# A linear recurrence with decay: chunks of 64 with the decay divided out, in place of block levels in chunks of 32

## The chip, the cores and the metric

The kernel runs on one core of a Trainium2 chip. A core has a matrix engine (TensorE, "PE" in the profile; its weight loads are "PEld"), a vector engine (VectorE, "DVE"), a scalar engine (ScalarE, "ACT"), GpSimd ("POOL") and SyncE ("SP"), which here only issues transfers. Each engine works its own list of instructions in order and waits on semaphores for the others. The metric is the device time of one execution in microseconds; less is better.

## The reference

For 4 sequences of 768 tokens and 8 heads of 40 channels, a state of 40 x 40 per head is carried over the tokens. The result of all heads is a row of 320 numbers per token, which then goes through two matrix products with a silu between them.

```python
for t in range(S):                                   # S = 768
    kt, vt, rt = (k[:, :, t], v[:, :, t], r[:, :, t])
    wt, at, bt = (w[:, :, t], a[:, :, t], b[:, :, t])
    y[:, :, t] = np.einsum('bhd,bhde->bhe', rt, state)
    Sa = np.einsum('bhde,bhe->bhd', state, at)
    state_decay = state * wt[:, :, None, :] - np.einsum('bhd,bhe->bhde', Sa, bt)
    state = state_decay + np.einsum('bhd,bhe->bhde', vt, kt)
...
h = x @ w_in                                         # (3072, 320) @ (320, 2048)
g = h * (1.0 / (1.0 + np.exp(-h)))
return (g @ w_out).astype(np.float32)                # (3072, 2048) @ (2048, 320)
```

The decays w are drawn between 0.85 and 0.95. All of it is float32; a float32 matrix product is two instructions on TensorE, a transpose one. The weights arrive as float64 and are put together to float32 on VectorE, nine instructions for each of 22 pieces (lines 126 to 134).

## The kernel before

A **unit** is 128 tokens of one sequence with all 8 heads. Two sequences are worked side by side, so a **group** is two units, and there are 12 groups. Channels lie on partitions, two heads of a pair in one tile (64 rows each, 40 used).

Inside a unit the recurrence is worked in 4 chunks of C = 32 tokens. What token s adds reaches token t through the product of the decays between them. That product is never formed by a quotient: each pair of tokens lies in one pair of sibling blocks of 1, 2, 4, 8 or 16 tokens (five **levels**), and each level has its own scaled copies of a, k and b. So the following stands once per level:

- `level` (lines 179 to 218): score products (line 191, weights of 128 columns), a masked copy on VectorE (line 195), transposes (line 207), and the scaling for the next level on GpSimd (lines 211 to 216);
- `read_level` (lines 365 to 402): products of r with v and u (line 375), a mask (line 382), the product with the keys (line 391), the scaling (line 399) and the sum (line 400).

Between them lie `by_token` (transposes, line 228, and line 232), `inverse` (forward substitution, 31 rows of two VectorE instructions each, lines 256 and 262, for the 64 chunks of two units on 64 partitions, with the scores going through memory before and the inverse after it), `solve` (lines 287 and 294, alternating head by head), and `chunk` (lines 308 to 355), which carries the state over the 4 chunks.

`moe` is the two matrix products (lines 423 and 440) with the sigmoid (line 431) and the product (line 432) for 256 tokens. `weave` spreads two lists of steps over each other: the rest of the group (from `inverse` on) with the `moe` of the group before. What engines do in the end is set by the scheduler, which moves independent instructions.

## Time and profile before

| | before |
|---|---|
| median of 3 runs | 3177.6 us (3167.85 to 3179.37) |
| span of the profiled execution | 3174.8 us |
| PE busy | 2888.6 us, 16992 matmul instructions |
| DVE busy | 1139.0 us |
| ACT busy | 482.0 us |
| POOL busy | 422.5 us |
| mean granted TensorE clock | 0.596 of full speed |

The span is what the profiled execution's instructions cover; it stands 2.8 us under the median. Busy time of PE is a union: overlapping matmuls count once. A row of instructions with "x" gives their number; a clock of 1.00 is 2.4 GHz and of 0.50 is 1.2 GHz.

### The profile page before, as it was taken

What the parts mean: (1) busy time and instruction counts of PE and PEld (TensorE: products, weight loads), DVE (VectorE), ACT (ScalarE), POOL (GpSimd) and SP (SyncE); (2) the same over time, 40 slices, a digit from 0 to 9 for tenths busy, and PEclk for the clock granted to TensorE, in tenths of its full rate; (3) what the DMA queues carried; (4) which work ended last, traced back from release to release, by engine and by line L of the source; (5) the groups of instructions that cost most, each with busy time, mean ns of one, the idle gap of its engine ahead of it and who ended that gap; (6) DMA issues with size and microseconds to landing.
All of it is one profiled execution on the core that took longest, in us unless ns stands there. A gap on an engine that the chain in (4) does not pass through costs nothing.

```text
span 3174.8 us, 40492 instructions
## 1 busy us (share of the span) xinstructions
PE 2888.6 (91%) x16992; PEld 2494.4 (79%) x16992; DVE 1139.0 (36%) x2146; ACT 482.0 (15%) x1058; POOL 422.5 (13%) x714
## 2 busy tenths in 40 slices
PE   8189989989989989998998998998999899899898
PEld 8178868958968968886896895897788689589686
DVE  5935423252251351342324225135034232422512
ACT  1001201111111111110120111111112012011111
POOL 4001101200300200210120030020011012003000
PEclk9555755575585575565566557557557555655757
DMA  3211101000010010000100000001001010000000
GB/s 86 75 40 43 27 11 29 27 11 9 23 36 5 25 36 5 27 27 11 29 27 11 24 22 21 5 25 31 9 27 29 9 29 27 11 20 13 15 1 9
DMA packets 103981, 75.56 MB, mean 24 GB/s; under 512 B 57976, under 2 KB 84344, under 8 KB 103800
## 3 DMA queue, kind: packets, MB, share of 16 engines
q1 hardware_dynamic: 100608, 62.16, 7.2%
q10 hardware_dynamic: 3192, 10.81, 1.2%
q8 instruction: 134, 2.20, 0.3%
q14 instruction: 47, 0.39, 0.0%
HBM read 58.79 MB, written 10.22 MB: 22 GB/s over the span
## 4 chain that ended last, share of the span: by engine, by line
PE 78%; DVE 17%; DMA 2%; SPq 1%; issue 1%; ACT 1%; POOL 0%; DVEq 0%; ACTq 0%; POOLq 0%
PE pm L191 23%; PE pg L336 11%; DVE tmp L256 8%; PE pl L375 7%; DVE XT L262 6%; PE pq L354 6%; PE pc L391 6%; PE pt L207 4%; PE pa L287 4%; PE pu L308 4%; PE pz L294 4%; PE pt L320 3%; PE ph L423 3%; PE pv L232 2%; PE pt L228 2%; DVE gts L432 1%
## 5 line engine op out<-in xcount | busy, mean ns | idle before, releaser
L191 PEld LDWEIGHTS pm<-a,kb 40*128 40x128 f32 x3840 | 733.4, 327 | 49.2 <-issue 28.9
L191 PE MATMUL pm<-a,kb 40*128 40x64 f32 x3840 | 758.1, 419 | 10.6 <-DMA a<-in_aT 9.1
L195 DVE COPY_PREDICATED MM<-mm_s,pm 128x512 f32<-128x512 int32 x240 | 227.5, 949 | 591.9 <-PE pm L191 591.9
L287 PE MATMUL pa<-XTb,at 128*64 128x128 f32 x384 | 132.0, 448 | 244.6 <-DMA XTb<-xd 244.6
L423 PE MATMUL ph<-xt,wi_s 120*128 120x256 f32 (+1 forms) x1152 | 289.0, 408 | 10.1 <-DMA xt<-mid 8.0
L423 PEld LDWEIGHTS ph<-xt,wi_s 120*128 120x128 f32 (+1 forms) x1152 | 224.5, 202 | 70.5 <-DVE gts L432 29.2
L327 POOL TENSOR_TENSOR gw<-G,tot 64x160 f32<-64x160 f32 x192 | 88.6, 461 | 1406.8 <-DVE G L346 1397.9
L256 DVE TENSOR_TENSOR tmp<-XT,mi 64x1 f32<-64x1 f32 (+30 forms) x372 | 272.5, 732 | 8.0 <-issue 0.3
L287 PEld LDWEIGHTS pa<-XTb,at 128*64 128x64 f32 x384 | 55.5, 206 | 263.9 <-issue 250.0
L375 PE MATMUL pl<-r,left 40*64 40x64 f32 x3840 | 245.7, 318 | 14.3 <-ACT left L369 14.3
L214 POOL TENSOR_TENSOR kb<-kb,tot 128x256 f32<-128x256 f32 x240 | 171.8, 716 | 586.2 <-PE pm L191 539.4
L375 PEld LDWEIGHTS pl<-r,left 40*64 40x64 f32 x3840 | 202.9, 216 | 44.3 <-ACT left L369 19.1
L311 DVE TENSOR_TENSOR U<-pu,zv 32x320 f32<-32x320 f32 x96 | 46.8, 487 | 499.7 <-PE pu L308 499.7
L440 PE MATMUL po<-wo_s,gts 128*128 128x320 f32 x768 | 209.7, 434 | 0.3
L346 DVE TENSOR_TENSOR G<-pg,gw 64x160 f32<-64x160 f32 x192 | 61.8, 322 | 399.8 <-PE pg L336 396.7
L336 PEld LDWEIGHTS pg<-v,kq 32*128 32x128 f32 x768 | 170.7, 323 | 31.7 <-issue 31.7
L440 PEld LDWEIGHTS po<-wo_s,gts 128*128 128x128 f32 x768 | 145.3, 190 | 63.1 <-DVE gts L432 4.3
L391 PE MATMUL pc<-lam,kt 128*64 128x64 f32 x1920 | 190.1, 324 | 3.2
L336 PE MATMUL pg<-v,kq 32*128 32x80 f32 x768 | 191.3, 427 | 0.0
L262 DVE TENSOR_REDUCE XT<-tmp 64x1 f32<-64x1 f32 (+30 forms) x372 | 184.2, 495 | 10.8
L354 PE MATMUL pq<-r,gt 128*128 128x32 f32 x768 | 184.1, 404 | 0.0
L336 PE MATMUL pg<-U,kq 32*128 32x80 f32 x768 | 183.5, 417 | 0.0
(63 smaller groups left out, 2689.0 us busy)
## 6 DMA issues: line engine op xcount, KB each, us to landing
kb<-in_bT SPq DMA_DIRECT2D x24, 256.0 KB
kb<-in_kT SPq DMA_DIRECT2D x24, 256.0 KB
a<-in_aT SPq DMA_DIRECT2D x24, 256.0 KB
tot<-in_wT SPq DMA_DIRECT2D x24, 256.0 KB
r<-in_rT SPq DMA_DIRECT2D x24, 256.0 KB
vu<-in_vT SPq DMA_DIRECT2D x24, 256.0 KB
room<-in_w_out ACTq DMA_DIRECT2D x10, 512.0 KB
room<-in_w_in ACTq DMA_DIRECT2D x8, 480.0 KB
```

Source lines behind the costliest of these rows:

```text
L191: nc.tensor.matmul(pm[:, c : c + 64], lhsT=u.kb[R, n, p, :], rhs=a_r[R, p], start=True, stop=True)
L195: nc.vector.copy_predicated(dst, mm_s[:, lv].bitcast(I32).rearrange("p (n l) -> p n l", l=L).unsqueeze(1).to_broadcast([128, H, 64 // L, L ...
L214: nc.gpsimd.tensor_tensor(out=k_l, in0=k_l, in1=totals(u.tot, lv, 1), op=ALU.mult)
L256: nc.vector.tensor_tensor(out=tmp[:, 0:t, 0:t], in0=XT[:, 0:t, 0:t], in1=mi[:, 0:t, t].unsqueeze(1).to_broadcast([NU * H * NC, t, t]), op= ...
L262: nc.vector.tensor_reduce(out=XT[:, 0:t, t], in_=tmp[:, 0:t, 0:t], axis=AX.X, op=ALU.add)
L287: nc.tensor.matmul(pa[DP * j : DP * j + DP, p * TT : p * TT + TT], lhsT=u.at[:, p, DP * j : DP * j + DP], rhs=x, start=True, stop=True,)
L336: nc.tensor.matmul(pg[:, p * 80 : p * 80 + 80], lhsT=u.kq[R, n, p, :], rhs=U[u.n][R, p, :, 0:D] if n else u.v[R, p * 80 : p * 80 + 80], st ...
L354: nc.tensor.matmul(pq[:, p * C : p * C + C], lhsT=gt[:, p, :], rhs=u.r[:, p, R], start=True, stop=True)
L375: nc.tensor.matmul(pl[64 * n : 64 * n + 64, p * 64 : p * 64 + 64], lhsT=left[R, n * P + p, :], rhs=halves(u.r, L)[1][R, p], start=True, st ...
L391: nc.tensor.matmul(pc[DP * j : DP * j + DP, p * 64 : p * 64 + 64], lhsT=u.kt[:, lv, p, DP * j : DP * j + DP], rhs=lam[:, j, p], start=True ...
L423: nc.tensor.matmul(ph[:, 0:T], lhsT=wi_s[0:n, k, f * 128 : f * 128 + 128], rhs=xt[0:n, k, :], start=k == 0, stop=k == 2,)
L440: nc.tensor.matmul(po[u.n][:, 0:DM], lhsT=gts[0][:, f, u.n * TT : u.n * TT + TT], rhs=wo_s[:, f, :], start=f == 0, stop=f == NF - 1,)
```

## The change

The levels go. A chunk is now C = 64 tokens, and a unit is 64 tokens of two sequences (`n` counts 12 steps of 64 tokens, `m` the two pairs of sequences), so that there are 24 units as before and the two sequences of a unit share the 128 partitions where tokens lie on partitions. For each unit a scan on VectorE forms the running product W of the decays, a reciprocal R = 1/W is taken, a is multiplied by W, and k and b by R (`scale`). Then one set of scores (`between`) serves the whole chunk, for b ahead of time and for k in `right`. The inverse of a 64 x 64 triangle is put together from its two 32 x 32 diagonal blocks, which `inverse` solves for four units at once on 128 partitions (6 times in all), and two small products in `merge`. The state is carried once per 64 tokens (`update`), and y is read out by one set of products (`read`, `write`).

Since 1/W could grow too large for other decays, the sums of squares of R and of W go to `chk`. At the end they are compared with 2^80, and if any is not below, a general version of the whole kernel, token by token on VectorE, runs behind a branch (lines 626 to 714 of the changed kernel). The weights' pieces come in another order, 9 of the 22 ahead of the first steps.

```diff
-C = 32
-LEVELS = (1, 2, 4, 8, 16)
-TT = 128
+TT = C = 64
+LIMIT = 2.0**80
...
-    def level(u, lv):
...
-    def read_level(u, lv):
...
+    def between(u, n, name, bufs):
+        s = sb.tile([128, 2, P, C], F32, name=name, bufs=bufs)
+        pm = [bank("pm") for _ in range(2)]
+        for p in range(P):
+            for be in range(2):
+                for j in range(2):
+                    q = P * be + p
+                    J = slice(DP * j, DP * j + DP)
+                    nc.tensor.matmul(
+                        pm[j][C * be : C * be + C, p * C : p * C + C],
+                        lhsT=u.kb[J, q, n, :],
+                        rhs=u.a[J, q, :],
...
+        def scale():
+            u.W = sb.tile([128, Q, C + 1], F32, name="W", bufs=6)
+            nc.vector.tensor_tensor_scan(
...
+            R = w[:, :, 1 : C + 1]
+            nc.vector.reciprocal(R, u.W[:, :, 1 : C + 1])
+            nc.gpsimd.tensor_tensor(out=u.a, in0=u.a, in1=u.W[:, :, 0:C], op=ALU.mult)
+            for n in (1, 0):
+                nc.gpsimd.tensor_tensor(out=u.kb[:, :, n], in0=u.kb[:, :, n], in1=R, op=ALU.mult)
+            junk = sb.tile([128, Q, C], F32, name="yx")
+            c = 2 * (NM * u.n + u.m)
+            nc.scalar.activation(out=junk, in_=R, func=AF.Square, accum_out=chk[:, c : c + 1])
...
     def inverse(md):
...
-        mi = sb.tile([NU * H * NC, C, C], F32, name="mi", tag="mid", bufs=2)
+        mi = sb.tile([128, 32, 32], F32, name="mi")
...
+    def merge(u, xd, zd):
...
     def chain(u, xt):
...
+        def read():
+            u.lam = sb.tile([128, 2, Q, C], F32, name="lam")
+            for j in range(2):
+                J = slice(DP * j, DP * j + DP)
+                pl = bank("pl")
+                for q in range(Q):
+                    nc.tensor.matmul(
+                        pl[:, q * C : q * C + C], lhsT=u.vut[J, q].rearrange("p n t -> p (n t)"), rhs=u.r[J, q, :], start=True, stop=True
+                    )
...
+        return [keys, right, solve] + ([] if last else [update]) + [read, write] + ([] if last else [turn])
...
+    load_w(units[0][0])
+    for u in units[0] + units[1]:
         load(u)
-    behind = load_weights()
-    for g in range(groups):
-        us = units[g]
-        for u in us:
+    ready = load_weights()
+    weave(prepare(0) + prepare(1), ready[0:9])
+    behind = ready[9:]
+    xt = None
+    for n in range(NN):
+        for u in units[n]:
             load_rv(u)
...
+        parts = [chain(u, xt) for u in units[n]]
+        steps = [x for pair in zip(*parts) for x in pair]
+        ahead = prepare(n + 2)
+        cut = len(behind) * 4 // len(steps)
+        weave(steps[0:4], behind[0:cut])
+        weave(steps[4:], behind[cut:], ahead)
+        behind = moe(n, xt)
     weave(behind)
...
+    flag = nc.values_load(bad[0:1, 0:1], min_val=0, max_val=1)
+    with tc.If(flag > 0):
```

The built programs show what becomes of this on the engines. A row is a line of the kernel, the operation, what it writes and reads, the shape of its output, and how many stand in a run. First TensorE before, in a middle group, from the last scores (L191) over `by_token` (L228, L232) and `moe` (L423, L440) to `solve` (L287, L294):

```order
L191 MATMUL pm<-a,kb 128x64 x16
L207 MATMUL pt<-ident,left 128x128 x4
L228 MATMUL pt<-ident,a 128x128 x4
L228 MATMUL pt<-ident,kb 128x128 x8
L232 MATMUL pv<-v,MM_75 128x40 x8
L423 MATMUL ph<-xt,wi_s 128x256 x48
L440 MATMUL po<-wo_s,gts 128x320 x32
L287 MATMUL pa<-XTb_76,at 64x128
L294 MATMUL pz<-mv,XTb_76 128x40
```

And TensorE after, in the second half of a step that has `moe` woven in (L516 and L533 are its two products; L463 is `read`, L476 and L483 are `write`, L284 is `merge`):

```order
L463 MATMUL pl<-r,vut 128x64 x16
L516 MATMUL ph<-xt,wi_s 128x256 x6
L463 MATMUL pl<-r,vut 128x64 x16
L533 MATMUL po<-wo_s,gts 128x320 x8
L476 MATMUL py<-r,GT_92 128x64 x8
L483 MATMUL py<-lam,kt 64x64 x16
L533 MATMUL po<-wo_s,gts 128x320 x4
L476 MATMUL py<-r,GT_93 128x64 x8
L483 MATMUL py<-lam,kt 64x64 x16
L533 MATMUL po<-wo_s,gts 128x320 x20
L516 MATMUL ph<-xt,wi_s 128x256 x46
L284 MATMUL pq<-XT_96,sb 32x32 x8
```

What stood in one piece, 48 and 32 products of `moe` followed by a product that needs the inverse, now stands in pieces of 3 to 8 products between those of the chain, and one long piece of 20 and 46 ahead of `merge`, which needs the inverse.

On the boundary between two steps after, TensorE has the transposes of `turn` (L452) and of `keys` (L341), then the scores (L185) and the products of `right` (L349, L361), with a few products of `moe` (L533):

```order
L483 MATMUL py<-lam,kt 64x64 x15
L452 MATMUL pt<-ident,Gbd_90 128x128 x4
L185 MATMUL pm<-a,kb 64x64 x16
L533 MATMUL po<-wo_s,gts 128x320 x2
L452 MATMUL pt<-ident,Gbd_91 128x128 x8
L533 MATMUL po<-wo_s,gts 128x320 x4
L341 MATMUL pt<-ident,kb 128x128 x16
L185 MATMUL pm<-a,kb 64x64 x16
L349 MATMUL pr<-Gbd_90,a 64x80 x8
L361 MATMUL pr<-v_2870,sk 64x40 x2
```

With the four of L452 that stand just ahead of these rows, 32 transposes lie on one boundary. Before, the nearest to it were the 24 of `by_token`, 12 for each unit with L232 between them.

On VectorE, at the start, the order after is the conversion of the pieces (L135 to L143), the scan and the reciprocal (L204, L213), the rows of the inverse (L247, L253), and only then the first mask of a chain step (L193 into `sk`):

```order
L140 SCALAR_TENSOR_TENSOR room<-room 120x512
L204 SCALAR_TENSOR_TENSOR W<-w,one 128x520
L142 TENSOR_TENSOR room<-room 120x512
L213 RECIPROCAL w<-W 128x8x64
...
L253 TENSOR_REDUCE XI<-tmp 128x31
L139 SCALAR_TENSOR_TENSOR room<-room 128x512
...
L143 ISA wo_s<-room 128x1024
L193 TENSOR_TENSOR sk<-pm,ms 128x256 x4
L436 TENSOR_TENSOR t<-pg,G_88 128x320
```

All 22 pieces stand ahead of that first mask; before, the pieces lay between the masked copies and the rows of the first group.

## Rows read from the trace of the kernel before

**Rows 1.** The page: engines' busy time, and the granted clock in 40 slices.

```profile
PE 2888.6 (91%) x16992; PEld 2494.4 (79%) x16992; DVE 1139.0 (36%) x2146; ACT 482.0 (15%) x1058; POOL 422.5 (13%) x714
...
PEclk9555755575585575565566557557557555655757
```

**Rows 2.** The page: the chain of work that ended last, shares by engine.

```profile
PE 78%; DVE 17%; DMA 2%; SPq 1%; issue 1%; ACT 1%; POOL 0%; DVEq 0%; ACTq 0%; POOLq 0%
```

**Rows 3.** Windows over one group: stretch, busy us of each engine (instructions), clock.

```profile
core 0: us, PE busy (x) PEld busy (x) DVE busy (x) ACT busy (x) POOL busy (x), PEclk, DMA share, GB/s
807.00:871.00 64.00, 64.00 (x320) 60.16 (x319) 16.27 (x18) 10.41 (x25) 18.54 (x29) 0.50 0.02 5
871.00:875.00 4.00, 4.00 (x20) 3.88 (x20) 0.72 (x1) 1.69 (x3) 1.80 (x3) 0.50 0.20 32
875.00:885.00 10.00, 10.00 (x70) 9.38 (x69) 1.27 (x3) 4.22 (x10) 2.98 (x2) 1.00 0.59 185
885.00:920.00 35.00, 34.71 (x138) 25.01 (x136) 32.83 (x69) 5.48 (x15) 0.00 (x0) 1.00 0.02 5
920.00:938.00 18.00, 2.80 (x10) 1.87 (x10) 8.71 (x7) 0.36 (x1) 0.00 (x0) 0.58 0.18 38
948.00:1015.00 67.00, 67.00 (x306) 58.87 (x306) 9.29 (x25) 7.54 (x17) 5.46 (x12) 0.50 0.02 5
1015.00:1050.00 35.00, 33.56 (x452) 28.77 (x454) 13.97 (x36) 8.31 (x15) 0.00 (x0) 0.50 0.10 25
```

**Rows 4.** Groups of instructions by line: busy us, mean ns of one.

```profile
L423 PE MATMUL ph<-xt,wi_s 120*128 120x256 f32 (+1 forms) x1152 | 289.0, 408 | 10.1 <-DMA xt<-mid 8.0 <-DVE gts L432 0.4
L256 DVE TENSOR_TENSOR tmp<-XT,mi 64x1 f32<-64x1 f32 (+30 forms) x372 | 272.5, 732 | 8.0 <-issue 0.3
L195 DVE COPY_PREDICATED MM<-mm_s,pm 128x512 f32<-128x512 int32 x240 | 227.5, 949 | 591.9 <-PE pm L191 591.9
L440 PE MATMUL po<-wo_s,gts 128*128 128x320 f32 x768 | 209.7, 434 | 0.3
L262 DVE TENSOR_REDUCE XT<-tmp 64x1 f32<-64x1 f32 (+30 forms) x372 | 184.2, 495 | 10.8
L382 DVE TENSOR_TENSOR lam<-pl,my_s 128x256 f32<-128x256 f32 x240 | 101.8, 424 | 111.9 <-PE pl L375 110.9
```

**Rows 5.** Timeline of TensorE at the boundary of the two clock levels: start, us, operation.

```profile
873.39 1.82 PE L228 MATMUL pt<-ident,kb 128*128 128x128 f32 x8
875.05 1.87 PE L232 MATMUL pv<-v,MM 128*128 128x40 f32 x16
...
935.20 0.66 PE L287 MATMUL pa<-XTb,at 128*64 128x128 f32 x2 [15.31 <-DMA XTb<-xd]
935.79 0.65 PE L294 MATMUL pz<-mv,XTb 128*128 128x40 f32 x2
936.37 0.69 PE L287 MATMUL pa<-XTb,at 128*64 128x128 f32 x2
```

**Rows 6.** Timeline of TensorE in another group, the same line at the lower level.

```profile
1385.35 3.47 PE L232 MATMUL pv<-v,MM 128*128 128x40 f32 x16
```

**Rows 7.** Windows over the start, of VectorE's instructions on the pieces of the weights.

```profile
0.00:300.00 300.00, 105.99 (x198) 0.66 0.23 65
```

**Rows 8.** TensorE's longest wait: total us, times, longest.

```profile
PE pa L287 <- DMA XTb<-xd: 244.6, 12, 76.6
```

**Rows 9.** Timeline of the end: last products, the transfer of y, the first of `moe`.

```profile
3118.17 12.14 SPq L408 DMA_DIRECT2D xt<-mid  x16
3118.61 1.70 PE L391 MATMUL pc<-lam,kt 128*64 128x64 f32 x16
3131.59 22.89 PE L423 MATMUL ph<-xt,wi_s 80*128 80x256 f32 x90 [0.26 <-DMA xt<-mid]
```

**Rows 10.** Timeline of the start: VectorE's first instruction on a piece.

```profile
9.24 0.43 DVE L126 TENSOR_SCALAR room<-room 120x512 int32<-120x512 int32 x1 [3.06 <-DMA room<-in_w_in]
```

More of the change, by code (lines that the diff above doesn't have):

```diff
@@ L357, in turn_u @@
[L357 to L374 removed]
+            nc.sync.dma_start(xd, XI)
@@ L453, in moe @@
         for f in range(NF):
             steps.append(partial(first, f))
-        for u in units:
+        for m in range(NM):
             for part in range(4):
-                steps.append(partial(second, u, part))
+                steps.append(partial(second, m, part))
         return steps
-    groups = (B // NU) * NT
-    units = [[unit(g, n) for n in range(NU)] for g in range(groups)]
-    for u in units[0]:
-        load(u)
-    behind = load_weights()
-    for g in range(groups):
-        us = units[g]
-        for u in us:
-            load_rv(u)
-        for lv in range(NL):
-            for u in us:
-                level(u, lv)
-        md = dr.tile([NU * H * NC, C, C], F32, name="md", bufs=2)
-        xd = dr.tile([NU * H * NC, C, C], F32, name="xd", bufs=2)
-        for u in us:
-            send_scores(u, md)
-        for u in us:
-            by_token(u)
-        xt = sb.tile([128, 3, NU * TT], F32, name="xt", bufs=2)
-        steps = inverse(md, xd)
-        steps += [partial(solve, u) for u in us]
-        steps += [partial(chunk, u, c) for c in range(NC) for u in us]
-        steps += [partial(turn_u, u) for u in us]
-        for lv in reversed(range(NL)):
-            steps += [partial(read_level, u, lv) for u in us]
-        steps += [partial(send_y, u, xt) for u in us]
-        if g + 1 < groups:
-            steps += [partial(load, u) for u in units[g + 1]]
-        weave(steps, behind)
-        behind = moe(us, xt)
@@ L490, with prepare, begin, do @@
-    weave(behind)
+    units = [[unit(n, m) for m in range(NM)] for n in range(NN)]
+    md = {}
+    def prepare(n):
+        if n >= NN:
+            return []
+        if n % 2 == 0:
+            md[0] = dr.tile([128, 32, 32], F32, name="md", bufs=2)
+        steps = [x for u in units[n] for x in pre(u, md[0])]
+        if n % 2 == 0:
+            return steps
+        box = {}
+        def begin():
+            box["rows"], box["xd"], box["zd"] = inverse(md[0])
+        steps.append(begin)
+        for i in range(32):
+            steps.append(lambda i=i: box["rows"][i]())
+        four = [(u, {}) for k in (n - 1, n) for u in units[k]]
+        for k, i in ((0, 0), (1, 0), (2, 0), (3, 0), (0, 1), (1, 1), (0, 2), (2, 1), (1, 2), (3, 1), (2, 2), (3, 2)):
+            def do(u=four[k][0], b=four[k][1], i=i):
+                if i == 0:
+                    b["s"] = merge(u, box["xd"], box["zd"])
+                b["s"][i]()
+            steps.append(do)
+        return steps
@@ new lines @@
+    weave(behind)
+    bad = const.tile([1, 1], I32, name="bad")
+    ok = sb.tile([128, 2 * NM * NN], F32, name="ok")
+    count = sb.tile([128, 1], F32, name="count")
+    ones = sb.tile([128, 1], F32, name="ones")
+    pb = bank("pb")
+    nc.vector.memset(ones, 1.0)
+    nc.vector.tensor_scalar(out=ok, in0=chk, scalar1=LIMIT, scalar2=None, op0=ALU.is_lt)
+    nc.vector.tensor_reduce(out=count, in_=ok, axis=AX.X, op=ALU.add)
+    nc.tensor.matmul(pb[0:1, 0:1], lhsT=count, rhs=ones, start=True, stop=True)
```

669 lines of the change are left out of this document (411 added, 258 removed).

## The prediction

> **What bounds the kernel now.** I read the page's shares first. TensorE is busy for 2888.6 of 3174.8 us, VectorE for 36% of the span, the others for less [rows 1]; and the chain that ended last lies on TensorE for 78% and on VectorE for 17% [rows 2]. So TensorE's list, in order, is the time, and VectorE counts where TensorE waits for it: it sits idle 244.6 us in 12 waits for the inverse [rows 8]. Next the windows over one group, which split the list by kind of work [rows 3]. The scores of the levels take 64 us with 320 instructions, 200 ns each; the chunks 67 us with 306, 219 ns each; the reading levels 33.56 us with 452, 74 ns each. The three differ little in arithmetic. The first two load weights of 128 columns for every instruction, the third of 64 columns, and alternate between the two halves of the columns. So **an instruction costs by its width: about 219 ns wide, 74 ns narrow**, whatever its product is worth. All three ran at a granted clock of 0.50, that is 1.2 GHz; `moe` ran at 1.00. The clock column is the second thing to see: it rises as the transposes of `by_token` have run, and falls in the window in which TensorE waits for the inverse. L232 shows what it is worth on wide instructions: 16 in 3.47 us at the lower level [rows 6], in 1.87 us at the higher [rows 5], a factor of 0.54.
>
> `moe` takes 289.0 and 209.7 us [rows 4], 499 in all; what is left of TensorE's busy time, 2390 us, is the recurrence.
>
> **The change on TensorE.** By the rows of the built program a unit has 64 score products after (L185), 64 in `merge`, 48 in `right`, 64 in `solve`, 32 in `update` and 32 narrow ones in `write`, counted as instructions: 304 narrow. Wide are 16 transposes, 32 in `read` and 16 in `write`: 64. Before, the recurrence had 15072 instructions, now 24 x 368 = 8832, and most of them narrow.
> - At the lower clock: 304 x 74 ns = 22.5 us and 64 x 219 ns = 14.0 us, 36.5 us a unit, 876 us in all, against 2390.
> - At the higher: the wide 14.0 x 0.54 = 7.6 us. No row shows narrow ones there; their bounds are half (11.3 us) and no gain (22.5 us), and I take 17, the middle. 24.6 us a unit, 590 in all.
> - Narrow products that differ in rows of the array alone, as half of L185 do, are not in the trace either. If these didn't overlap, some 100 a unit would cost up to twice 74 ns, 7 us a unit; if four ran side by side, less than 74. I leave 74.
>
> `moe` stays at 499 us.
>
> **The other engines.** The rows of the inverse cost (272.5 + 184.2) / 12 = 38 us a time [rows 4]; with 128 partitions filled they come 6 times, not 12: 228 us of VectorE gone. The masked copies go (227.5 us). A mask of 128x256 costs 0.42 us [rows 4]; four a unit, two of double size and the rest make some 9 us a unit with the scan and the reciprocal. These two the trace doesn't show: an instruction over 512 elements takes between 0.7 us (0.42 scaled from 256) and the 0.95 us of the masked copy [rows 4], and with twice that for a serial operation I take 1.3 us each. VectorE comes to 24 x 9 + 228 + 79 for `moe` + 106 = about 630 us. It stays under TensorE. The Trainium skill ("VectorE: DVE Perf Modes", First, the fixed hardware budget) says that reciprocal is an iterative divide with a repeat count of 8; an estimate by that page is 4.3 us for 512 elements, which would add some 15 us to the start below and nothing elsewhere. No row here shows it.
>
> **The start loses its cover.** This is the part that speaks against the change. VectorE needs 106 us for the weights [rows 7], which lay beside TensorE's long scores. Now all 22 pieces stand ahead of the first mask of a step in VectorE's order, and so do the first inverse (38), five scans and reciprocals (13), eight masks (3.4); its first piece lands at 9.2 us [rows 10], and the clearing of buffers takes 3. Sum 173 us, in which TensorE only has the scores and merges of four units, 4 x 96 x 74 ns = 28 us.
>
> **Waits.** The transfer of y takes SyncE 12.14 us for a group [rows 9] and `moe` of the same step stands right behind it; 20 to 24 products of 0.54 us each are ahead of it in one kind of step, transposes in the other, which covers most. Changes of shape cost too: L287 and L294, two and two, take 1.17 us for four [rows 5], 292 ns each against 219, or 0.15 us a change, and a step has some 25 more changes than the rows that I took prices from. I put 7 us on each of 11 steps, 77 in all. The wait for the inverse mostly goes, since 40 products of L533 and 92 of L516 (some 34 us) stand ahead of `merge`.
>
> **The end.** From the last narrow product's start to dense `moe` it took 13 us [rows 9]; I take 11 from its end, 3 for the last store, and 5 (a guess) to read the flag and branch past the general version: 19.
>
> **The sum.** 173 + 848 (876 less the 28) + 499 + 77 + 19 = **1616 us with the recurrence at 1.2 GHz**, and with 571 (590 less 19) in place of 848 **1339 us at 2.4 GHz**. Which? In the window 875 to 885 the clock had risen behind 12 transposes and stayed up through L232 [rows 3, 5]; the fall comes where TensorE idles. After the change the long idle is gone, and each step's boundary has 32 transposes, so I expect the higher level for two thirds of the recurrence: 1616 - 185 = 1431. The span stands 2.8 us under the median of the runs, which is nothing here: **1430 us**.
>
> A rule of the Trainium skill speaks against that step: "TensorE: Matmul & The Clock Gate", Part 4, says that transposes don't count as a busy array and don't bring the full clock. By it the boundary would not lift the clock, and the sum would lie near 1616. The trace disagrees: at 875 us the level was 1.00 and only the levels' work and the transposes of L228 stood ahead of it [rows 3, 5].
>
> **Rivals.**
> 1. *The clock stays high and narrow products halve.* For it: no fall in the trace with TensorE at work. Against: long stretches of narrow and wide work stayed at 0.50. Time: 173 + 24 x (7.6 + 11.3) - 14 + 499 + 96 = 1208, up to 1339.
> 2. *The clock stays low,* since the pieces of `moe` are too short between the steps of the chain. The woven part of `moe` then doubles too: 48 and 12 of 96 and 64 products per two steps, 30.7 us, 5.5 times, 169 us. Time 1616 to 1785.
> 3. *VectorE's queue.* In each second step the masks of `read` and the scaling of y stand behind rows of the inverse. TensorE has some 30 us of work ahead of them; if that were not so, up to 38 us in each of 6 steps: 1430 + 228 = 1660 at most. The Trainium skill ("TensorEngine Tiling (Array Packing)", Key Properties) says that a change of tiling mode drains the array, which would work in the same direction; the 0.15 us a change of L287 and L294 agrees, and 46 changes a step by 12 would be 83 us, of which the sum has about half.
> 4. *The other side: the general version runs.* It decides at a sum of squares of 2^80 = 1.2e24. With decays of 0.85 and more, 64 of them give 1/W of at most 33,000, and 512 squares 5.6e11, so the branch should not be taken. If it were, 768 tokens by 9 VectorE operations of some 0.5 us (0.42 for 256 elements, here 400) would add 3500 us: about 5000, slower.
>
> **How the numbers follow.** The mixed clock, 1340 to 1560: 0.5. Rival 1: 0.17. Rival 2: 0.2. Rival 3 alone: 0.1. Rival 4: 0.03. The range takes in rival 1 from its lower end and rivals 2 and 3 to the middle: 1210 to 1700, about 0.8. A difference of 0.5% is what a measurement of this kernel can tell from none; here all cases but the last are far beyond it: faster 0.96, same 0.01, slower 0.03.
>
> **What would show it.** TensorE with about 10750 matmul instructions and still the engine of the last chain; narrow runs (L185, L383, L483) near 74 ns an instruction where the clock is 0.50; a first L516 no sooner than 200 us; a granted clock between 0.7 and 0.9 over the span; no wait over 10 us for the inverse past the start. Wrong would be: a clock near 0.5 throughout, narrow products at over 100 ns, or waits of TensorE for VectorE in every step.

## The result, and the profile after

| | before | after |
|---|---|---|
| median | 3173.74 us (3167.85 to 3179.37) | **1168.44 us** (1157.89 to 1178.94, 4 runs) |
| ratio, 95% interval | | **0.3671** [0.3651, 0.3692] |
| span of the profiled execution | 3174.8 us | 1156.1 us |
| mean granted clock | 0.596 | 0.929 |

The change makes the kernel 2.7 times as fast. The forecast was 1430 us with a range from 1210: the direction is right, the size is not, and the time lies below the whole range, near the lower end of rival 1 (1208). The ratio leaves out the run of 1178.94 us, which counts as a slow one.

The page of the kernel after: busy time, the granted clock in 40 slices, and the chain that ended last. They answer to [rows 1, 2].

```profile
PE 938.7 (81%) x10674; PEld 763.6 (66%) x10674; DVE 622.7 (54%) x1037; ACT 267.7 (23%) x652; POOL 137.4 (12%) x138
...
PEclk9999998799998998997999997998988999979899
...
PE 54%; DVE 25%; SPq 9%; DMA 7%; issue 2%; ACT 1%; POOL 1%; DVEq 0%; ACTq 0%; POOLq 0%
```

TensorE is still first, with 10674 instructions (about 10750 were forecast), but no longer for nine tenths of the span. The clock column is the surprise: before, its digits were mostly 5, now they are 7 to 9.

The windows show where TensorE is idle (columns as in [rows 3]):

```profile
0.00:177.00 177.00, 17.62 (x398) 16.52 (x399) 166.09 (x288) 19.08 (x45) 39.40 (x40) 1.00 0.47 116
177.00:240.00 63.00, 57.05 (x918) 50.19 (x917) 25.75 (x38) 18.09 (x43) 9.47 (x10) 0.81 0.38 93
240.00:520.00 280.00, 263.32 (x3037) 210.82 (x3036) 153.02 (x250) 76.75 (x190) 33.89 (x32) 0.94 0.28 67
520.00:1085.00 565.00, 539.44 (x6020) 439.21 (x6020) 268.28 (x443) 145.94 (x356) 54.60 (x57) 0.92 0.25 61
1085.00:1156.10 71.10, 61.26 (x308) 46.82 (x307) 9.52 (x21) 7.85 (x20) 0.00 (x0) 0.93 0.06 15
```

In the first 177 us VectorE works for 166 and TensorE for 18. After that TensorE idles 48 us up to 1085 (the lengths less the busy times) and 10 us in the last window.

The groups by line, which answer to [rows 4]: seven of TensorE's and four of VectorE's. The "mean ns" of TensorE's rows counts overlapped instructions in full, so the price of one is the busy time divided by the count.

```profile
L516 PE MATMUL ph<-xt,wi_s 120*128 120x256 f32 (+1 forms) x1152 | 305.7, 416 | 44.6 <-DVE gts L525 21.3 <-DMA xt<-yx 20.1 <-issue 1.7
L533 PE MATMUL po<-wo_s,gts 128*128 128x320 f32 x768 | 229.7, 449 | 0.0
L463 PE MATMUL pl<-r,vut 64*128 64x64 f32 x768 | 81.9, 282 | 0.0
L476 PE MATMUL py<-r,GT 128*128 128x64 f32 x384 | 66.8, 348 | 0.0
L185 PE MATMUL pm<-a,kb 64*64 64x64 f32 x1536 | 43.2, 235 | 72.9 <-POOL kb L216 72.9
...
L421 PE MATMUL pg<-vu,kt 128*64 128x40 f32 x704 | 24.2, 230 | 0.7 <-issue 0.7
L401 PE MATMUL pw<-XT,RHS 64*64 64x64 f32 x768 | 21.2, 225 | 0.0
...
L247 DVE TENSOR_TENSOR tmp<-XI,mi 128x1 f32<-128x1 f32 (+30 forms) x186 | 138.6, 745 | 4.2 <-DMA mi<-md 0.7
L253 DVE TENSOR_REDUCE XI<-tmp 128x1 f32<-128x1 f32 (+30 forms) x186 | 93.4, 502 | 3.9
L213 DVE RECIPROCAL w<-W 128x512 f32<-128x512 f32 x24 | 80.3, 3347 | 0.8
...
L204 DVE TENSOR_TENSOR_SCAN W<-w,one 128x520 f32<-128x520 f32 x24 | 30.7, 1278 | 6.6 <-DMA w<-in_wT 6.0 <-DVE sk L193 0.3
```

43.2 us for 1536 products of L185 is 28 ns each, 28 for L401, 34 for L421; the wide L463 and L476 stand at 107 and 174. All nine narrow lines together come to 263 us for 7232 instructions, 36 ns each.

The timeline of TensorE in one step without `moe` (start, us, line); its last row is L476 in another step, one with `moe`:

```profile
684.25 2.29 PE L421 MATMUL pg<-vu,kt 128*64 128x40 f32 x64
686.47 0.69 PE L185 MATMUL pm<-a,kb 64*64 64x64 f32 x32
687.10 6.80 PE L463 MATMUL pl<-r,vut 64*128 64x64 f32 x64
693.83 3.67 PE L476 MATMUL py<-r,GT 128*128 128x64 f32 x16
...
599.90 1.90 PE L476 MATMUL py<-r,GT 128*128 128x64 f32 x16
```

And the windows of the same stretch, for the clock:

```profile
687.00:692.40 5.40, 5.40 (x70) 5.33 (x63) 4.09 (x7) 0.00 (x0) 2.31 (x4) 1.00 0.56 136
692.50:706.10 13.60, 13.60 (x107) 12.68 (x106) 6.48 (x5) 0.59 (x1) 0.02 (x1) 0.50 0.32 74
```

32 products of L185, which go round the four quarters of the array, take 0.69 us, 22 ns each. And the clock falls at 692.5 us although TensorE is busy without a gap in both windows: in the wide run of L463, so that 16 of L476 take 3.67 us and elsewhere 1.90.

### The profile page after: what moved, and what is told of

It is laid out like the page before. It is cut to its first block, busy times and chain, and to the rows that moved or that the text cites. A ratio compares the mean times of both kernels' runs of the same rounds, so it can differ in the third digit from the quotient of the medians.

```text
span 1156.1 us, 25310 instructions
## 1 busy us (share of the span) xinstructions
PE 938.7 (81%) x10674; PEld 763.6 (66%) x10674; DVE 622.7 (54%) x1037; ACT 267.7 (23%) x652; POOL 137.4 (12%) x138
## 4 chain that ended last, share of the span: by engine, by line
PE 54%; DVE 25%; SPq 9%; DMA 7%; issue 2%; ACT 1%; POOL 1%; DVEq 0%; ACTq 0%; POOLq 0%
PE ph L516 17%; PE po L533 10%; SPq L498 7%; DVE tmp L247 7%; PE pl L463 6%; DVE XI L253 4%; DVE w L213 4%; PE py L476 4%; DMA xt<-yx 2%; PE pq L284 2%; PE pg L421 2%; PE py L483 2%; PE pm L185 2%; DVE gts L525 2%; PE pt L452 2%
## 5 line engine op out<-in xcount | busy, mean ns | idle before, releaser
L516 PE MATMUL ph<-xt,wi_s 120*128 120x256 f32 (+1 forms) x1152 | 305.7, 416 | 44.6 <-DVE gts L525 21.3
L516 PEld LDWEIGHTS ph<-xt,wi_s 120*128 120x128 f32 (+1 forms) x1152 | 225.5, 205 | 101.1 <-DVE gts L525 34.8
L533 PE MATMUL po<-wo_s,gts 128*128 128x320 f32 x768 | 229.7, 449 | 0.0
L533 PEld LDWEIGHTS po<-wo_s,gts 128*128 128x128 f32 x768 | 145.0, 195 | 55.8 <-issue 3.9
L525 DVE TENSOR_TENSOR gts<-ph,sg 128x256 f32<-128x256 f32 x192 | 80.0, 420 | 174.5 <-ACT sg L524 174.1
L247 DVE TENSOR_TENSOR tmp<-XI,mi 128x1 f32<-128x1 f32 (+30 forms) x186 | 138.6, 745 | 4.2 <-DMA mi<-md 0.7
L524 ACT ACTIVATE sg<-ph 128x256 f32<-128x256 f32 x192 | 73.0, 383 | 219.1 <-PE ph L516 211.3
L216 POOL TENSOR_TENSOR kb<-kb,w 128x512 f32<-128x512 f32 x48 | 69.8, 1477 | 415.8 <-DVE w L213 244.8
L284 PE MATMUL pq<-XT,sb 32*32 32x32 f32 x768 | 34.8, 200 | 91.6 <-DMA XT<-zd 91.6
L185 PE MATMUL pm<-a,kb 64*64 64x64 f32 x1536 | 43.2, 235 | 72.9 <-POOL kb L216 72.9
L284 PEld LDWEIGHTS pq<-XT,sb 32*32 32x32 f32 x768 | 29.8, 114 | 109.0 <-DVE wo_s L143 85.2
L193 DVE TENSOR_TENSOR sk<-pm,ms 128x256 f32<-128x256 f32 x48 | 18.2, 419 | 152.5 <-PE pm L185 147.7
L253 DVE TENSOR_REDUCE XI<-tmp 128x1 f32<-128x1 f32 (+30 forms) x186 | 93.4, 502 | 3.9
L185 PEld LDWEIGHTS pm<-a,kb 64*64 64x64 f32 x1536 | 34.1, 142 | 84.8 <-POOL kb L216 75.2
L463 PE MATMUL pl<-r,vut 64*128 64x64 f32 x768 | 81.9, 282 | 0.0
L463 PEld LDWEIGHTS pl<-r,vut 64*128 64x128 f32 x768 | 78.9, 194 | 4.5 <-issue 4.1
L213 DVE RECIPROCAL w<-W 128x512 f32<-128x512 f32 x24 | 80.3, 3347 | 0.8
L476 PEld LDWEIGHTS py<-r,GT 128*128 128x128 f32 x384 | 65.2, 261 | 3.3
L476 PE MATMUL py<-r,GT 128*128 128x64 f32 x384 | 66.8, 348 | 0.0
L214 POOL TENSOR_TENSOR a<-a,W 128x512 f32<-128x512 f32 x24 | 29.3, 1222 | 310.7 <-DMA a<-in_aT 221.6
```

The source lines that it names most:

```text
L185: nc.tensor.matmul(pm[j][C * be : C * be + C, p * C : p * C + C], lhsT=u.kb[J, q, n, :], rhs=u.a[J, q, :], start=True, stop=True,)
L213: nc.vector.reciprocal(R, u.W[:, :, 1 : C + 1])
L247: nc.vector.tensor_tensor(out=tmp[:, 0:t, 0:t], in0=XI[:, 0:t, 0:t], in1=mi[:, 0:t, t].unsqueeze(1).to_broadcast([128, t, t]), op=ALU.mult,)
L253: nc.vector.tensor_reduce(out=XI[:, 0:t, t], in_=tmp[:, 0:t, 0:t], axis=AX.X, op=ALU.add)
L284: nc.tensor.matmul(pq[be][r + 32 : r + 64, h * 32 : h * 32 + 32], lhsT=u.sb[r : r + 32, h // P, h % P, 32:64], rhs=X[r : r + 32, h, 32:64] ...
L463: nc.tensor.matmul(pl[:, q * C : q * C + C], lhsT=u.vut[J, q].rearrange("p n t -> p (n t)"), rhs=u.r[J, q, :], start=True, stop=True)
```

## The experiments

Ratios are to the kernel before on the same chip, medians in us. Each diff is against the changed kernel unless it says otherwise.

### The changed kernel again, and without its guard

> The changed kernel once more, beside the next three on one chip: 1157 to 1179 us, as its runs so far. Both theories expect the same.

Measured: **1173.01** (1160.37 to 1193.93), ratio 0.3696 [0.3688, 0.3704].

```diff
-            nc.scalar.activation(out=junk, in_=R, func=AF.Square, accum_out=chk[:, c : c + 1])
-            nc.scalar.activation(out=junk, in_=u.W[:, :, 1 : C + 1], func=AF.Square, accum_out=chk[:, c + 1 : c + 2])
...
-    flag = nc.values_load(bad[0:1, 0:1], min_val=0, max_val=1)
-    with tc.If(flag > 0):
```

> The guard left out: no sums of squares, no flag, no general version behind a branch. My term for it was 5 us, a guess: 5 to 10 us less than the changed kernel, all of it at the end, since the sums of squares lie beside other work. Rival: the general version weighs on the whole program (more code, larger span): 20 us less or more. No change at all would say that the branch is free.

Measured: **1181.57**, 0.3732 [0.3712, 0.3752]. The guard costs nothing that shows; without it the kernel is about 1% slower, which neither forecast had, with a clock of 0.921 against 0.928 and TensorE busy 9 us longer. What ties that to the Squares taken from ScalarE stays open. Rival 4 of the prediction was settled by the result: the general version doesn't run.

### The order over the quarters of the array

```diff
-        for p in range(P):
-            for be in range(2):
-                for j in range(2):
+        for be in range(2):
+            for j in range(2):
+                for p in range(P):
```

(and the same in `merge`, `right`, `solve`, `update` and `write`)

> The products of the recurrence stay as they are, only their order in a run changes: a run of the scores, of the right sides, of the solve, of the update and of the write first does all products of one quarter of the array (or one half), then those of the next, where the changed kernel goes round over the quarters. Theory: a narrow product costs little because its neighbours lie in other quarters and overlap with it. Then L185 rises from 28 ns each to some 54 or more, L401 from 28 too, L421 and L483 from 34 and 52 to 60 or more, TensorE is busy 120 us longer, and the time is 1290 us (1250 to 1400). Rival: the price of a product follows from its width and the clock alone, whoever its neighbour is; then no line's mean moves by over 10 ns and the time stays within 1% of 1170 us.

Measured: **1281.31**, 0.4043 [0.4019, 0.4067]. Groups by line of this run:

```profile
L185 PE MATMUL pm<-a,kb 64*64 64x64 f32 x1536 | 80.6, 233 | 61.6 <-POOL kb L216 61.6
...
L483 PE MATMUL py<-lam,kt 128*64 128x64 f32 x768 | 58.3, 260 | 0.0
...
L421 PE MATMUL pg<-vu,kt 128*64 128x40 f32 x704 | 38.3, 230 | 0.0
L401 PE MATMUL pw<-XT,RHS 64*64 64x64 f32 x768 | 36.9, 224 | 0.0
L284 PE MATMUL pq<-XT,sb 32*32 32x32 f32 x768 | 35.0, 200 | 88.8 <-DMA XT<-zd 88.8
```

The same products in another order: L185 goes from 28 to 52 ns, L401 to 48, L421 to 54, L483 to 76; the nine narrow lines from 263 to 392 us, the time up by 113 us, at the same mean clock (0.928). The theory holds: a narrow product is cheap because its neighbour works in another quarter. The rival falls. One of the nine lines does not follow: L284 (products of 32 x 32) changed its order too and stays at 45 to 46 ns each (34.8 us before); no run here shows why.

```diff
-        for p in range(P):
-            for be in range(2):
-                for j in range(2):
+        for j in range(2):
+            for p in range(P):
+                for be in range(2):
...
-            for p in range(P):
-                for j in range(2):
+            for j in range(2):
+                for p in range(P):
```

> Two lines change their order. In the scores (L185) neighbours differ only in the columns of the array that they write through, the rows of contraction change half way through a run; in L401 neighbours differ only in the rows. Everything else is as in the changed kernel, where both go round over all four quarters. Theory of the prediction's upper bound (rows alone give no overlap, columns do): L185 goes from 28 to about 27 to 40 ns, L401 from 28 to 54 ns or more, the time rises by 20 us to about 1190. Rival: rows overlap as columns do, both lines stay between 25 and 40 ns and the time stays within 10 us.

Measured: **1188.72**, 0.3751 [0.3724, 0.3778]. The two lines among the groups of this run:

```profile
L185 PE MATMUL pm<-a,kb 64*64 64x64 f32 x1536 | 53.7, 235 | 63.1 <-POOL kb L216 26.0 <-DMA vu<-in_v 19.8 <-DMA kb<-in_kT 17.0
...
L401 PE MATMUL pw<-XT,RHS 64*64 64x64 f32 x768 | 23.4, 224 | 0.0
```

With neighbours that differ in columns only L185 costs 35 ns, with neighbours that differ in rows only L401 costs 30; in the same quarter it was 52 and 48, over all four 28. So the theory falls in its main point: rows alone overlap as well as columns, and both together best. That the time rose by 16 to 20 us over the two medians of the changed kernel, as the theory said, is no support: 11 us are L185's, and the clock was lower (0.915).

### The wide lines made narrow

```diff
-                pl = bank("pl")
...
-                        pl[:, q * C : q * C + C], lhsT=u.vut[J, q].rearrange("p n t -> p (n t)"), rhs=u.r[J, q, :], start=True, stop=True
+            pl = [bank("pl") for _ in range(2)]
+            for q in range(Q):
+                for n in range(2):
+                    for j in range(2):
...
+                            pl[j][C * n : C * n + C, q * C : q * C + C], lhsT=u.vut[J, q, n, :], rhs=u.r[J, q, :], start=True, stop=True
...
-                    py[:, q * C : q * C + C], lhsT=gt[:, q, :], rhs=u.r[:, q, :], start=q == 0, stop=False,
+                    py[J, q * C : q * C + C], lhsT=gt[J, q, J], rhs=u.r[J, q, :], start=q == 0, stop=False,
```

> The 32 wide products of read (about 106 ns each) become 64 narrow ones that go round the four quarters of the array, and the 16 wide ones of write 32 narrow ones on its two diagonal quarters. Theory (price by width and by order over the quarters): narrow ones cost 20 to 30 ns, so read falls from 3.4 to about 1.5 us a unit and the state product from 1.9 or more to about 0.8; 45 to 80 us less in all, 1090 to 1125 us, and the 14 us stretches at a clock of 0.50 in every second step go or shrink. Rival (an instruction has its price whatever its width, about what one at the higher clock costs): 48 more of them a unit, no gain or up to 30 us more. Second rival: gain swallowed by waits on VectorE, under 20 us.

Measured: **1129.29**, 0.3552 [0.354, 0.3564]. The two split lines among the groups of this run:

```profile
L480 PE MATMUL py<-r,GT 64*64 64x64 f32 x768 | 29.3, 225 | 2.3 <-issue 2.3
L464 PE MATMUL pl<-r,vut 64*64 64x64 f32 x1536 | 28.9, 221 | 5.1 <-issue 4.2 <-DVE t L436 0.9
```

L463's 768 wide products and L476's 384 become 1536 and 768 narrow ones, 19 and 38 ns each, that take 28.9 and 29.3 us in place of 82.9 and 66.8 (the changed kernel's repeat). Of these 91 us 44 arrive at the end, 4 us short of the theory's range: `moe` waits 36.4 us for the transfer of y in place of 20.5, L483 (L487 in this run) now 16.2 us for VectorE's masks, and the mean clock stays at 0.928.

> Half of the run with the narrow read: only L463 (64 rows, 128 columns, x768) is split into products of one quarter each, the wide product of L476 stays. Theory: the two parts of that gain add up by their busy time, 54 us of 91 here, so the time is about 1147 us (1135 to 1158). Rival: the gain of the two hangs on the clock, which falls in the wide run that the read and L476 make together; then L476 alone keeps the fall and the time stays within 10 us of 1173.

Measured: **1122.05**, 0.3535 [0.3527, 0.3544], the fastest version that leaves nothing out. Groups by line of this run (L464 is `read`, L478 the wide product of `write`):

```profile
L478 PE MATMUL py<-r,GT 128*128 128x64 f32 x384 | 49.4, 285 | 0.0
...
L464 PE MATMUL pl<-r,vut 64*64 64x64 f32 x1536 | 28.4, 220 | 6.4 <-issue 6.0 <-DVE t L436 0.4
```

And one of its waits (total us, times, longest):

```profile
PE ph L518 <- DMA xt<-yx: 35.4, 19, 4.4
```

Neither theory nor rival: the half does all of the gain. The product that was not touched went from 66.8 to 49.4 us, 174 to 129 ns, since it now runs mostly at the higher level; the mean rose from 0.928 to 0.946. Splitting it too takes another 20 us off its line, but the clock is back at 0.928 and TensorE's busy time nearly the same (865.6 and 867.7 us). TensorE's busy time fell by 74 us here and the time by 51: the wait of `moe` for the transfer of y grew from 20.5 to 35.4 us.

```diff
-                    nc.tensor.transpose(out=pt[:, c : c + 128], in_=u.kb[:, q].rearrange("p n t -> p (n t)"), identity=ident)
+                        nc.tensor.matmul(
+                            pt[j][C * n : C * n + C, q * DP : q * DP + DP],
+                            lhsT=u.kb[J, q, n, :], rhs=ident[J, J], start=True, stop=True,
+                        )
...
+                    nc.tensor.matmul(pt[J, q * DP : q * DP + DP], lhsT=gbd[J, q, j, :], rhs=ident[J, J], start=True, stop=True)
```

> The narrow read and write of the earlier run, and the turns of the keys (L341) and of the state (L452) as products of one quarter with the identity in place of 128 by 128 transposes; of the state only the two diagonal quarters are turned, since the others are zero and nobody reads them. Theory: L341 goes from 30.5 to some 21 us and L452 from 24 to some 10 us, and the time from 1129 to about 1105 us (1095 to 1115). Rival: TensorE is no longer what ends last there (VectorE's masks and the transfers of the output are waited for), and the time stays within 10 us of 1129.

Measured: **1151.99**, 0.3631 [0.3623, 0.3639]: 23 us slower than without it. Both lines of the turns in this run:

```profile
L342 PE MATMUL pt<-ident,kb 64*64 64x64 f32 x1536 | 34.0, 248 | 4.2 <-issue 3.3 <-DVE sb L193 0.8
...
L458 PE MATMUL pt<-ident,Gbd 64*64 64x64 f32 x704 | 25.6, 221 | 0.0
```

Both the theory and its rival (within 10 us of 1129) fall. The counts show the slip: a float32 product is two instructions, a transpose one, so 192 transposes became 1536 instructions, not 768, and the line rose from 30.5 to 34.0 us; the turn of the state went from 24.0 to 25.6. The rest of the 23 us is not pinned to a line. The mean clock without a single transpose is 0.931, with them 0.928.

### The same two causes in the kernel before

```diff
-                    nc.tensor.matmul(
-                        pm[:, c : c + 64], lhsT=u.kb[R, n, p, :], rhs=a_r[R, p], start=True, stop=True
-                    )
+                    for half in range(2):
+                        S = slice(64 * half, 64 * half + 64)
+                        nc.tensor.matmul(
+                            pm[S, c : c + 64], lhsT=u.kb[R, n, p, S], rhs=a_r[R, p], start=True, stop=True
+                        )
```

> The kernel before, with one change: each of its 3840 products of L191 (128 columns of the array) is split in two products of 64 columns that stand next to each other in the run. Theory: a narrow product beside one in another quarter or half is cheap also in the kernel before, and it is width and order, not the chunk length, that made the recurrence of the changed kernel cheap; 7680 products of about 54 ns (415 us) in place of L191's 758 us make about 2830 us (2780 to 2900). Rival, the price that the prediction used: each narrow product costs 74 ns at the lower clock whatever stands beside it, so the split saves 190 us at most (2980 or more), and if the price is by the instruction it costs up to 750 us (3900).

Measured: **2811.24**, 0.8859 [0.8842, 0.8876]. The split line among the groups of this run:

```profile
L193 PE MATMUL pm<-a,kb 40*64 40x64 f32 x7680 | 404.2, 312 | 15.7 <-DMA a<-in_aT 8.0 <-POOL a L213 5.5 <-POOL kb L183 1.9
```

and the same line, with L375, in the kernel before:

```profile
L191 PE MATMUL pm<-a,kb 40*128 40x64 f32 x3840 | 758.1, 419 | 10.6 <-DMA a<-in_aT 9.1 <-POOL a L211 1.4
L375 PE MATMUL pl<-r,left 40*64 40x64 f32 x3840 | 245.7, 318 | 14.3 <-ACT left L369 14.3
```

Twice the instructions in half the time: 52.6 ns each, at the lower clock, where L191 took 197. With the chunk length unchanged, 363 us come off. The prediction's 74 ns was too much already at 1.2 GHz.

```diff
-            for p in range(P):
-                for n in range(2):
+            for n in range(2):
+                for p in range(P):
```

> The kernel before, with the loops of one line (L375, 3840 products of 64 columns) changed so that neighbours write through the same columns for a whole run, where they alternate between the two halves. Theory: alternation hides half of each; without it the line goes from 64 to about 107 ns each, and the time rises by some 165 us to 3340 (3270 to 3380). Rival: the order of columns makes no difference to the line; 3175 us within 1%.

Measured: **3244.68**, 1.0240 [1.0198, 1.0282]. Two groups by line of this run:

```profile
L375 PE MATMUL pl<-r,left 40*64 40x64 f32 x3840 | 357.1, 317 | 14.3 <-ACT left L369 14.3
...
L423 PE MATMUL ph<-xt,wi_s 120*128 120x256 f32 (+1 forms) x1152 | 272.5, 391 | 9.2 <-DMA xt<-mid 7.0 <-DVE gts L432 0.2
```

The line goes from 245.7 to 357.1 us, 64 to 93 ns (107 expected), so the rival falls; but only 70 of these 111 us reach the time. In this trace L423 (289.0 in the trace of the kernel before), L232 and L228 take 37 us less in all, at a mean clock of 0.645 against 0.596. That is not the change's doing: of its four runs two have a mean of 0.601 and 0.602 and take 3244 and 3241 us, two have 0.645 and 0.643 and take 3246 and 3267; and the kernel before on the same chip has five runs at 0.596 or 0.597 (3175 to 3178 us) and two at 0.641 (3169 and 3174). The two traces come from runs of different kinds in this respect, in either kernel. Where the missing 41 us went stays open.

### What holds the clock

> The feed-forward stage does about a sixteenth of its products (its output is not the reference's); the recurrence is as in the changed kernel and now stands nearly alone on TensorE. Theory: with narrow products in all quarters the recurrence by itself keeps TensorE busy and holds the higher level of the clock (mean 0.8 or more); the span is 640 to 720 us. Rival, the prediction's case: it is the long products of the feed-forward stage that lift the clock; without them the mean is below 0.65 and the span 850 us or more.

Measured: **1068.2** (one run), mean clock 0.68. Its steady part, as one window:

```profile
300.00:1060.00 760.00, 482.98 (x7270) 426.98 (x7270) 322.91 (x465) 158.17 (x370) 77.61 (x78) 0.61 0.27 66
```

The theory falls. The span is nearly that of the whole kernel: with `moe` down to 67 us on TensorE from 535, 100 us come off. The recurrence alone runs at 0.61, but it also leaves TensorE idle for 36% of this window, two thirds of that for the inverse (186 us). So idle time was still a rival, and part of it was taken away:

```diff
-            steps.append(partial(row, t))
+            steps.append(partial(row, t) if t < 3 else lambda: None)
```

> As the run with a sixteenth of the feed-forward products, and the inverse does two of its 31 rows (the output is not the reference's), so that VectorE has some 36 us less to do for each inverse and TensorE hardly waits for it past the start. Theory: it was idle time that kept the clock down there; with the chain's products close together the mean past the start rises to 0.8 or more, and the span falls by more than the waits taken away, to 650 us or less. Rival: the long products of the feed-forward stage are what lifts the clock; it stays at 0.5 to 0.68 past the start, and the span is 780 us or more.

Measured: **879.46** (one run). A window of the steady part:

```profile
300.00:800.00 500.00, 379.51 (x5697) 333.63 (x5690) 135.75 (x188) 126.19 (x300) 70.88 (x72) 0.62 0.36 88
```

TensorE's busy share goes from 64% to 76%, the clock from 0.61 to 0.62. A quarter of the window is still idle, but the same trace has a stretch with no gap, here whole and in three parts:

```profile
502.90:561.20 58.30, 58.28 (x963) 53.37 (x962) 17.69 (x21) 21.40 (x50) 10.76 (x10) 0.65 0.36 81
503.00:522.50 19.50, 19.50 (x327) 17.27 (x328) 0.12 (x1) 10.91 (x25) 2.31 (x2) 0.50 0.51 108
523.00:536.00 13.00, 12.98 (x384) 12.41 (x380) 6.10 (x7) 4.84 (x13) 4.67 (x4) 1.00 0.35 95
536.50:556.50 20.00, 20.00 (x158) 18.30 (x158) 5.88 (x11) 2.62 (x6) 3.78 (x4) 0.50 0.24 54
```

The mean is 0.65 there too, against 0.92 for the changed kernel between 520 and 1085 us, where TensorE is busy for 95%. So idle time is not what kept it down; the products of `moe` between those of the recurrence are what holds the higher level, as the rival says. The parts show that the recurrence has both levels by itself: the higher one in the narrow products that go round the quarters, up to the middle of the wide run of L463, and the lower one behind that, in `write`, and in the first part (`merge` and transposes).

### What the start waits for

```diff
-    ready = load_weights()
-    weave(prepare(0) + prepare(1), ready[0:9])
-    behind = ready[9:]
+    weave(prepare(0) + prepare(1))
+    behind = load_weights()
```

(with a buffer shared between the first inverse and the pieces, so that these come after it)

> All 22 pieces of the weights wait for the end of the first inverse (their buffer is held by its scratch tile till then). Theory (the start is VectorE's queue, and the conversion is the part that can move): the first transposes of a step come at 80 to 100 us, not 174, the first products of moe at about 170 us or a little later than before, and the time falls by 30 to 70 us, to 1100 to 1140. Rival (the start only moves, since moe waits for the weights all the same and VectorE has the same work in its first 250 us): less than 15 us.

Measured: **1192.07**, 0.3761 [0.3752, 0.3771]. My theory fell: 19 us slower. The start in windows of this run:

```profile
0.00:177.00 177.00, 40.26 (x848) 37.67 (x848) 120.62 (x191) 24.26 (x58) 32.92 (x45) 0.96 0.42 100
177.00:300.00 123.00, 94.36 (x866) 77.06 (x867) 95.92 (x199) 19.52 (x46) 10.55 (x11) 0.71 0.35 90
```

and of the changed kernel's repeat:

```profile
0.00:177.00 177.00, 18.28 (x404) 16.90 (x405) 167.93 (x291) 19.56 (x45) 39.40 (x40) 1.00 0.47 116
177.00:300.00 123.00, 114.27 (x1380) 95.52 (x1380) 69.76 (x120) 27.81 (x69) 18.15 (x18) 0.88 0.31 76
```

The chain starts at 145 us in place of 173, and TensorE does 444 instructions more by 177. But VectorE then converts the pieces, 63 us of them between 145 and 222, and TensorE waits some 23 us for masks and scalings of VectorE; the first product of `moe` comes at 223 us and not at 218. It does 514 instructions fewer in the second window, and that one at 0.71 of the clock instead of 0.88. The work is moved, not hidden.

```diff
-            ts(out=e, in0=hi, scalar1=20, scalar2=0x7FF, op0=shr, op1=ALU.bitwise_and)
...
-            nc.vector.tensor_tensor(out=dst.bitcast(I32), in0=e, in1=lo, op=ALU.add)
+            nc.vector.tensor_tensor(out=dst.bitcast(I32), in0=hi, in1=hi, op=ALU.bitwise_or)
```

> The conversion of each piece of the weights is one operation in place of nine, so that the weights of the feed-forward stage are not the reference's and VectorE is free of some 90 us of its work ahead of the first keys. Theory: VectorE's work is what the start waits for; the first keys come at some 90 us in place of 174, and the time falls by 60 to 90 us (1080 to 1110). Rival: pieces, decays and inverse wait for their DMAs and for each other, so the start falls by at most 30 us; or the start falls but TensorE then waits elsewhere or gets the lower clock, as with the later weights: under 30 us come off the end.

Measured: **1153.66** (1143.79 to 1167.88), 15 to 19 us under the two medians of the changed kernel, and its lowest run 14 to 17 us under theirs. The rival held: VectorE has 78 us less to do, but the first keys (L333 here) come at 157 us, since VectorE now waits ahead of that for pieces (28 us) and for decays (12 us) to arrive. The instructions of L333, with their first and last start:

```profile
L333 PE MATMUL pt<-ident,kb x192: 270/273/474, 157.1 to 1036.9; 128*128 128x128 f32 x192
```

(the same edit of the inverse as above, with `moe` whole)

> The changed kernel with two of the 31 rows of each inverse (the output is not the reference's), the feed-forward stage whole. Theory: only the first inverse stands open, so the first keys come 36 us earlier, at some 138 us, and since the later ones lie beside TensorE's work the time falls by 20 to 40 us to about 1140. Rival: as with the one-operation conversion the start waits for something else (the decays' transfers and the pieces of the weights), or TensorE waits later for the weights, and less than 15 us come off.

Measured: **1084.65** (one run), far more than either said. The keys, with first and last start, and then `moe`'s first product among the groups by line:

```profile
L341 PE MATMUL pt<-ident,kb x192: 270/272/474, 121.9 to 975.9; 128*128 128x128 f32 x192
```

```profile
L516 PE MATMUL ph<-xt,wi_s 120*128 120x256 f32 (+1 forms) x1152 | 313.4, 419 | 19.5 <-DVE gts L525 11.4 <-ACT ot L542 4.7 <-DMA xt<-yx 3.1
```

The start is 52 us shorter, not 36: with the rows gone, 26 us of the pieces' conversion stand behind the first keys, where it was 5 us. And `moe` waits 19.5 us in all in place of 44.6. The waits that went are those for `gts` and for the transfer of y, 41.4 us before and 14.5 now. So the rows of the inverse are not free past the start either: on VectorE they stood in the way of both. As the order of the conversion changed along with the rows, the run does not tell what the rows alone are worth to the start.

## Why the prediction was wrong, by its own steps

| term | predicted | measured | from |
|---|---|---|---|
| start | 173 | 177 | first keys at 174.0 us, the window ends behind them |
| recurrence | 663 | 386 | TensorE's busy time past 177 us, 921, less `moe` |
| `moe` | 499 | 535 | L516 and L533, 305.7 + 229.7 |
| waits | 77 | 48 | idle between 177 and 1085 us |
| end | 19 | 10 | idle in the last window |
| sum | 1431 | 1156 | |

**The step that failed is the price of a narrow product**: "their bounds are half (11.3 us) and no gain (22.5 us), and I take 17, the middle", together with "if four ran side by side, less than 74. I leave 74." Measured are 263 / 24 = 11.0 us a unit, over both levels of the clock, so it lies even below the bound for the higher level alone. The prediction's mixture, a third at 22.5 and two thirds at 17, makes 452 us for 24 units; the missing 189 us are most of the recurrence's 277. The run in one quarter's order gives 392 / 24 = 16.3 us: 17 is right for products whose neighbours stand in the same quarter. The upper end came from 74 ns, the mean of a window of the reading levels in which L375 takes 64 ns each, L391, a line of another shape, 103, and 14 wide instructions stand as well; the split of the scores in the kernel before shows 52.6 ns at the same clock.

The Trainium skill ("TensorEngine Tiling (Array Packing)", Key Properties) says that different tiles can execute weight loads and matrix products in parallel. The trace agrees, with 22 ns for each of 32 products in four quarters. The order of `between` was readable in the diff; the prediction saw the case and kept the price that leaves it out.

**The clock**, "the higher level for two thirds of the recurrence": that left 283 us (a third of 848) at 1.2 GHz. A mean of 0.929 over 1156 us means 164 us at the lower level (0.071 / 0.5 of the span), `moe`'s share included. The direction was right, and its stated mechanism was wrong twice. "The fall comes where TensorE idles" fails at 692.5 us, where it fell in a gapless run of wide products. That the 32 transposes of a boundary keep the level up fails in the runs with a sixteenth of `moe`, which have all of them and stay near 0.61, and in the run with the turns as products, which has none and a mean of 0.931. Rival 2's ground, that pieces of `moe` between the steps are too short to hold the clock, is refuted by the result's 0.929 and by the runs with a sixteenth of `moe`: the pieces are what holds it. The Trainium skill ("TensorE: Matmul & The Clock Gate", Part 4), which the prediction set aside, says that transposes don't bring the full clock. The runs agree that they are not needed for it (0.931 without any), but not that they never go ahead of it: the rise at 522.5 us in the stretch above comes 1.3 us behind 16 transposes, and the one at 875 us in the kernel before, behind 12, stays unexplained.

**Rival 1** came nearest, 1208 against 1168: narrow products at 11.3 us a unit, and a high clock. The 11.3 is right by luck: it is half of 74 ns for the clock alone, while the runs show a price that hangs on the neighbour, 36 ns over all narrow lines and 54 in one quarter's order at the same mean clock. Its waits and end of 96 us measured 58.

**Wide products** were nearly right: 202 us measured, 234 by the mixture. A further 62 us of the recurrence is that the lines' busy times add up to 1000 us and TensorE's to 938.7: lines overlap each other as well, which the sum did not allow for. With 4 us less of the recurrence inside the start, 189 + 31 + 62 - 4 make the 277 but for rounding.

**The start** was right in part by luck. Six scans and six reciprocals take 27.5 us ahead of the first keys, where 13 was put for five of each; against that the first piece comes at 5.5 us and not at 9.2, and lines of VectorE overlap, which the sum did not allow for. The reciprocal takes 3.35 us, not the 1.3 taken; the estimate of 4.3 us from what the Trainium skill ("VectorE: DVE Perf Modes", First, the fixed hardware budget) says was nearer, above the measurement. The scan at 1.28 us was right. That VectorE's work of the start adds up in a row is what the trace shows (166 of 177 us busy), yet it is not what the start alone waits for: the one-operation conversion takes 78 us of VectorE's work away and 17 us of the start.

**Waits and `moe`** are off by 29 and 36 us in opposite directions. The 77 us held shape changes, which would count as busy time and not as idle, so what they cost stays open; and woven pieces of `moe` cost more than the dense ones before (535 us against 499). Rival 3 (VectorE's queue) did not come in its form, 6.5 us of waits for the inverse past the start, but the run without the inverse's rows shows that VectorE's order costs some 25 us of `moe`'s waits.

## What to carry to other kernels

Price a small matrix product by what stands next to it in the engine's order: the same float32 product of one quarter of the array cost 52 ns behind its own quarter and 28 when the loop went round all four, so write the loop over heads innermost or outermost by that, and split a wide product whose halves can go round. Look for the clock in the mixture of work: long products woven between short ones kept the higher level (a mean of 0.92 with TensorE busy for 95%) where the short ones alone did not (0.65 in a stretch without a gap). And when an engine off the path is emptied ahead of a start, ask what else arrives only then; two of three attempts on the start here moved all or most of the wait instead of removing it.

## What the runs showed of the hardware that was not expected

- The clock fell to 1.2 GHz in the middle of 64 wide products on 64 rows with TensorE busy for 5.40 of 5.40 us ahead of it and 13.60 of 13.60 behind, and splitting just these products took the untouched line behind them from 174 to 129 ns each.
- Neighbours in other rows of the array overlap as those in other columns do: 30 and 35 ns, against 48 and 52 in the same quarter.
- In the same program the mean clock can differ from run to run with hardly a change of the time: the kernel before has runs at 0.597 that take 3175 to 3178 us and runs at 0.641 that take 3169 and 3174.
